# Batch 0 of a fused attention and feed-forward kernel: head groups share their last keys in pairs, and the load order changes

## The chip, the cores and the metric

One core of one Trainium2 chip. The metric is the device time of the whole program in microseconds. Three runs of the kernel before took 389.02, 389.39 and 390.98; the median is 389.39. The profiled execution took 389.4, and its span from the first to the last instruction is 387.6.

## What is computed

Softmax attention over 8 batches, 12 heads, 448 tokens and head size 64, then a feed-forward layer with SiLU on the tokens of all heads put side by side.

```python
scores = (1 / sqrt(64)) * q @ k.T          # per batch and head: 448 x 448
attn   = exp(scores - max) / sum           # softmax over the keys
x      = (attn @ v), heads side by side    # 3584 tokens x 768
h      = x @ w_in                          # 768 x 2048
g      = h / (1 + exp(-h))                 # SiLU
out    = g @ w_out                         # 2048 x 768, float32
```

## The kernel before, in words

**Units.** The 12 heads of a batch are three groups of four heads. For one group the keys and queries come in as one load each (`load_k`, L298, tile rk; `load_q`, L303, tile rq), 224 KB in float16, cast on the way by a DMA that POOL issues. VectorE turns both (`turn_k`, L347, tile KT; `turn_q`, L368, in place): 32 x 32 blocks are transposed, so that the head dimension lies on the partitions. The keys of a group lie in four chunks of up to 128.

**Score bursts.** `scores` (L419) multiplies one chunk of keys with the queries. Each head needs two matmuls of 32 rows (even and odd parts of the head dimension), so one burst is 8 matmuls of 448 queries on PE; heads run side by side on strips of 32 rows. The result s is 128 keys x 4 heads x 448 queries in PSUM, in two halves of two heads. `expo` (L439) turns each half into E with one exponential on ScalarE. Thus one burst gives two exponentials of 128 x 896.

**Lone and paired groups.** 448 keys are three and a half chunks. In a *lone* group (`LONES`, the first four: all of batch 0 and the first group of batch 1) the chunks have 128, 128, 96 and 96 keys, which makes four bursts. The other groups go in *pairs*: the first of a pair is "low", the second "high"; each has three chunks of 128 keys, and one burst takes the last 64 keys of both (`scores_rest`, L428: 16 matmuls with 64 key columns). A pair has seven bursts. In AV the shared E is read by both groups, with zeros in V in the 64 rows of the other one; POOL clears those rows (L323).

**Sums and AV.** For each group the sums of E over the keys (lone: matmuls with ones, `attend_part` L524 and `attend_wide` L494; pair: VectorE first adds three E into T, L455, then `attend_sums` L478) and two parts of E times V (16 matmuls of 32 columns each) go into PSUM tiles a. VectorE makes the inverse (`inverse`, L532: transpose sT, reciprocal, transpose rdn) and multiplies (`norm`, L567), which gives xT.

**Batch 0 in halves.** `BEGIN` lists the units of batch 0: group 0 with query columns 0 to 7 (of 14, 32 queries each), group 1 the same, group 2 whole, then the second halves of groups 0 and 1. A half unit packs two key chunks into one burst, so it has two bursts. As soon as all three groups have their first seven columns, the feed-forward of those tokens can start.

**Feed-forward.** `ffn1` (L609) makes h from xT and w_in, for batch 0 in two pieces of 224 tokens, six matmuls for each block of 128 columns of w_in; ScalarE makes tanh (L630), VectorE the gate G. Then batch 0's first products with w_out follow (o), and later batches go through sums of blocks with fewer products (p, f).

**What sets the order.** The kernel is written by a planner that runs when the program is built: class `Order` with a list of operations for each engine, their supposed durations, due times and rings of buffers. It decides which operation is written next on PE (a score burst, AV or feed-forward), and when nothing is ready in the first stage it writes filler: matmuls on a tile of zeros (`run_zeros`, L1618). The engines then run their own lists in order. The loads stand in one list on POOL, in the order of the `plan_...` calls; at most eight are in flight. There are 3 rk, 4 rq, 3 KT, 9 E and 2 V buffers, and 3 half-burst s tiles. Two PSUM banks hold sums and AV until batch 0's scores are done (`hand_over`), then four.

Of the kernel before, what the change touches and what calls it, by code (L numbers as in the profile page):

```python
# [20 lines left out]
OVERLAP = {"ACT": 0.09, "DVE": 0.07}  # L21
LOADS, DMA_SLOW = 8, 1.45
# [3 lines left out]
DMA_TAIL = 1.5  # L26
# [77 lines left out]
class Order:  # L104
# [48 lines left out]
    def step(self):  # L153
# [26 lines left out]
        elif self.pool:  # L180
# [9 lines left out]
            if at is not None and at <= self.now:  # L190
                self.pool.pop(0)
                if ring is not None:
                    ring.take()
                self.start(op)
                self.sent.append(op)
                took += DMA_SLOW if len(self.sent) == 3 else 0.0
                self.dma_free = max(self.dma_free, self.now + DMA_START) + took
                op.done = self.dma_free + DMA_TAIL
# [7 lines left out]
def kernel(  # L206
# [18 lines left out]
    KROWS = (128, 128, 96, 96)  # L225
    X_TOK = {
        "lone": ((0, 4), (4, 4), (8, 4), (12, 2)),
# [9 lines left out]
    LONES = (0, 1, 2, 3)  # L237
# [3 lines left out]
    NEAR, LATE = 0.15, -0.9  # L241
    COLD, FIRST = 8.5, 47
# [5 lines left out]
    WIDE_SUMS = True  # L248
    BEGIN = ((0, 0, 7), (1, 0, 7), (2, 0, 14), (0, 7, 14), (1, 7, 14))
    NB0 = len(BEGIN)  # L250
# [30 lines left out]
    for i in range(2):  # L281
        nc.vector.memset(both[64 * i : 64 * (i + 1)], 0.0)
        nc.vector.memset(both[64 * i : 64 * (i + 1), 16 * i : 16 * (i + 1)], 1.0)
    w_in_t = const.tile([128, NDC, DFF], FP16, name="w_in_t")
# [18 lines left out]
    def load_q(n):  # L303
        b, hg, g0, g1 = units[n]
        t = sb.tile([128, (g1 - g0) * D], FP16, name=f"rq_{n}", tag="rq", bufs=NRQ)
        nc.gpsimd.dma_start(out=t, in_=group_of(q, b, hg)[:, D * g0 : D * g1])  # L306
        rawq[n] = t

    def form(b, hg):
        n = NG * b + hg  # L310
        if n in LONES:
            return "lone"
        return ("low", "high")[(n - sum(x < n for x in LONES)) % 2]


    def load_v(b, hg0, hg1, x):
# [4 lines left out]
        if x == 0 and kind != "lone":  # L321
# [9 lines left out]


# [35 lines left out]
    def turn_q(n):  # L368
        t = rawq[n][:].bitcast(FP32).rearrange("p (g i) -> p g i", i=32)
# [33 lines left out]
    def score(pS, n, c, e, h, x0, x1, p0):  # L403
        b, hg, g0, g1 = units[n]
        nq = 32 * (g1 - g0)
        at = nq * (c % per_burst(n))
        nc.tensor.matmul(  # L407
            out=pS[p0 : p0 + 32 * (x1 - x0), h % 2, at : at + nq],
            lhsT=KT[(b, hg)][32 * h : 32 * (h + 1), c, x0:x1, :, e],
            rhs=QT[n][32 * h : 32 * (h + 1), e],  # L410
# [3 lines left out]

# [4 lines left out]
    def scores(n, w, ys):  # L419
        score_banks(n, w, ys)  # L420
        for c in range(per_burst(n) * w, per_burst(n) * (w + 1)):
            for e in range(2):
                for y in ys:
                    for h in (2 * y, 2 * y + 1):
                        score(pS_t[(n, w, y)], n, c, e, h, 0, rows_of(n, c) // 32, 0)


# [8 lines left out]
    def rows_of(n, c):  # L436
        return KROWS[c] if form(*units[n][:2]) == "lone" else 128

    def expo(n, w, y):  # L439
        kr = rows_of(n, w * per_burst(n))  # L440
        nk = 32 * (units[n][3] - units[n][2]) * per_burst(n)
        if (n, w) not in E:
            E[(n, w)] = sb.tile([128, HG, S], FP16, name=f"E_{n}_{w}", tag="E", bufs=NE)
        nc.scalar.activation(  # L444
            out=E[(n, w)][0:kr, 2 * y : 2 * y + 2, 0:nk],
            in_=pS_t[(n, w, y)][0:kr, :, 0:nk],
# [4 lines left out]

    def add_e(n, step):
        if step == 0:
            T[n] = sb.tile([128, HG, S], FP16, name=f"T_{n}", tag="T", bufs=NT_)
# [7 lines left out]
    def attend_mm(a, n, part, c, h, k0, k1, e, start, stop):  # L462
        b, hg, g0, g1 = units[n]
        nq = 32 * (g1 - g0)
        at = nq * (c % per_burst(n))
        if part == 0:
            w = ones[k0:k1, :]
        else:
            w = VT[b][k0:k1, HG * hg + h, c, part - 1 :: 2]
        nc.tensor.matmul(  # L470
            out=a[32 * h : 32 * (h + 1), 0:nq],
            lhsT=w,
            rhs=e[k0:k1, h, at : at + nq],
# [20 lines left out]
    def attend_wide(n):  # L494
        a = acc[(n, 0)] = psum_bank(f"a_{n}_0")
        for w in range(2):
            k = rows_of(n, 2 * w)
            for h in range(HG):
                nc.tensor.matmul(
                    out=a[32 * h : 32 * (h + 1), 0:S],  # L500
                    lhsT=ones[0:k, :],
                    rhs=E[(n, w)][0:k, h, 0:S],
                    start=(w == 0),
                    stop=(w == 1),
                )

    def attend(ns, part, n):
        if part == 0 and per_burst(n) == 2:
            attend_wide(n)
            return  # L510
        if part == 0 and len(ns) == 2:
            attend_sums(ns)
            return
        if part < 3:
            acc[(n, part)] = psum_bank(f"a_{n}_{part}")
        else:
            acc[(n, 3)] = acc[(n, 1)] = psum_bank(f"a_{n}_3")
            acc[(n, 2)] = acc[(n, 1)][:, 256:512]
            attend_part(ns, 1, n)
            attend_part(ns, 2, n)  # L520
            return
        attend_part(ns, part, n)

    def attend_part(ns, part, n):  # L524
        for c in range(NCH):
            e = E[(ns[0] if c == NCH - 1 else n, c // per_burst(n))]
            for h in range(HG):
                attend_mm(
                    acc[(n, part)], n, part, c, h, 0, rows_of(n, c), e, c == 0, c == NCH - 1
                )  # L530
# [1188 lines left out]
```

## Time and profile before

| | us |
|---|---|
| median of three runs | 389.39 |
| the profiled execution | 389.4 |
| its span | 387.6 |
| PE busy | 379.7 |
| DVE busy | 272.2 |
| ACT busy | 250.4 |
| POOL busy | 90.7 |

In the profile PE is TensorE, DVE is VectorE, ACT is ScalarE. A line of the page's slices has 40 digits, each the busy share of 9.7 us in tenths. A line of the timeline gives start, length, engine, line of the kernel, operation, tiles and shapes, and in brackets how long the engine was idle before it and what ended that. Matmuls overlap, so the lengths of neighbours on PE add up to more than the time from one start to the next; start to start is what a matmul costs. Tiles: rk and rq are raw keys and queries, KT turned keys, s scores, E exponentials, a sums and AV, xT the attention result, h and th the feed-forward, z the spare bank that filler writes.

### The profile page before, as it was taken

The page shows a single profiled execution, that of the slowest core. Times are in us where ns is not written, and L with a number is a line of the kernel's source. Part 1 is how long each engine was busy: PE and PEld are TensorE (multiplying, and loading weights), DVE is VectorE, ACT ScalarE, POOL GpSimd, SP SyncE. Part 2 cuts the span into 40 slices and gives each one's busy share as a digit, 9 for nine tenths or more (in the row PEclk, how much of TensorE's full clock was granted, in tenths as well). Part 3 has the DMA queues.
Part 4 walks back from the last instruction along what each step waited for, and adds up shares of the span by engine and source line. Part 5 has one row for each costly group of instructions (what it writes and reads, how often), then busy time and mean ns, then how long its engine had stood idle before and what let it go on. Part 6 is the DMA issues. An engine that isn't in the chain of part 4 may idle for free.

```text
span 387.6 us, 10639 instructions
## 1 busy us (share of the span) xinstructions
PE 379.7 (98%) x4374; PEld 198.8 (51%) x4374; DVE 272.2 (70%) x550; ACT 250.4 (65%) x383; POOL 90.7 (23%) x175
## 2 busy tenths in 40 slices
PE   8989999999999999999999999999999999999995
PEld 3548765444454444454455454554445655555663
DVE  2666768899985787978697658567769965447441
ACT  4988873787766879675955667566783248882220
POOL 7633366407006432502443024000000000000000
PEclk9999999999999999999999999999999999999999
DMA  7999999909148662924964139002000130001333
GB/s 115 199 210 209 166 159 214 202 5 126 20 102 121 126 85 34 155 57 84 149 91 56 42 82 160 4 3 65 20 1 2 43 100 23 0 2 41 91 96 101
DMA packets 36001, 34.52 MB, mean 89 GB/s; under 512 B 11376, under 2 KB 35184, under 8 KB 35952
## 3 DMA queue, kind: packets, MB, share of 16 engines
q0 software_dynamic: 25456, 22.82, 40.2%
q1 hardware_dynamic: 10080, 10.53, 10.1%
q8 instruction: 34, 0.56, 0.6%
q10 hardware_dynamic: 416, 0.49, 0.4%
q14 instruction: 15, 0.12, 0.1%
HBM read 45.61 MB, written 11.01 MB: 146 GB/s over the span
## 4 chain that ended last, share of the span: by engine, by line
PE 84%; DMA 12%; POOL 2%; issue 1%; DVE 1%; ACT 0%; POOLq 0%
PE p L598 31%; PE h L598 24%; PE s L407 8%; PE f L598 8%; PE a L470 8%; DMA rq<-in_q_dram 4%; DMA w_out_t<-in_moe_w_out_dram 3%; DMA rk<-in_k_dram 2%; DMA V<-in_v_dram 2%; PE a L486 2%; PE o L598 2%; POOL V L325 1%; POOL rk L300 0%; POOL rq L306 0%; POOL w_in_t L334 0%
## 5 line engine op out<-in xcount | busy, mean ns | idle before, releaser
L444 ACT ACTIVATE E<-s 128x896 f16<-128x896 f32 (+1 forms) x172 | 148.1, 915 | 31.1 <-PE s L407 30.4
L598 PE MATMUL h<-xT,w_in_t 128*32 128x448 f16 (+2 forms) x1338 | 117.2, 339 | 0.0
L598 PEld LDWEIGHTS <-w_in_t 128*32 128x32 f16 (+1 forms) x1410 | 71.8, 97 | 56.1 <-issue 11.6
L630 ACT ACTIVATE th<-h 128x448 f16<-128x448 f32 x96 | 52.3, 546 | 35.9 <-PE h L598 31.8
L598 PEld LDWEIGHTS <-G 128*128 128x128 f16 (+1 forms) x532 | 43.0, 98 | 33.2 <-issue 5.2
L889 ACT COPY ost<-p 128x384 f32<-128x384 f32 x52 | 25.0, 480 | 51.5 <-PE p L598 44.3
L674 DVE SCALAR_TENSOR_TENSOR G<-th,h 128x448 f16<-128x448 f16 (+1 forms) x80 | 44.1, 557 | 16.2 <-ACT th L630 15.8
L325 POOL DMA_DIRECT2D V<-in_v_dram x88 | 48.3, 560 | 15.5 <-DMA w_out_t<-in_moe_w_out_dram 6.1
L598 PE MATMUL p<-w_out_t,G 128*128 128x384 f16 (+1 forms) x304 | 49.1, 326 | 0.0
L407 PE MATMUL s<-rq,KT 32*128 32x448 f16 (+4 forms) x736 | 45.2, 345 | 1.5 <-DVE rq L378 1.3
L598 PEld LDWEIGHTS <-S 128*128 128x128 f16 (+1 forms) x384 | 29.8, 98 | 23.2 <-issue 3.1
L470 PE MATMUL a<-E,V 128*32 128x448 f16 (+3 forms) x800 | 39.9, 342 | 0.7 <-DVE sT L537 0.7
L306 POOL DMA_DIRECT2D rq<-in_q_dram x26 | 14.5, 557 | 101.6 <-PE s L407 89.4
L598 PE MATMUL p<-D,S 128*128 128x384 f16 (+1 forms) x256 | 36.8, 326 | 0.0
L895 DVE TENSOR_TENSOR ost<-p,ost 128x384 f32<-128x384 f32 x39 | 21.5, 552 | 14.5 <-PE p L598 12.4
L470 PEld LDWEIGHTS <-V 128*32 128x32 f16 (+1 forms) x832 | 20.7, 97 | 18.4 <-issue 6.1
L407 PEld LDWEIGHTS <-KT 32*128 32x128 f16 (+2 forms) x832 | 13.1, 98 | 29.9 <-issue 26.5
L586 DVE SCALAR_TENSOR_TENSOR xT<-a,rdn 128x448 f16<-128x448 f32 x44 | 26.4, 616 | 2.8 <-PE a L470 1.6
L455 DVE TENSOR_TENSOR T<-T,E 128x1792 f16<-128x1792 f16 x20 | 21.7, 1086 | 8.4 <-ACT E L444 8.4
L455 DVE TENSOR_TENSOR T<-E,E 128x1792 f16<-128x1792 f16 x20 | 21.7, 1083 | 8.3 <-ACT E L444 8.3
L360 DVE STREAM_TRANSPOSE KT<-rk 128x256 f32<-128x256 f32 (+3 forms) x48 | 16.5, 382 | 11.2 <-DMA rk<-in_k_dram 10.3
L598 PE MATMUL p<-w_out_t,S 128*128 128x384 f16 (+1 forms) x128 | 19.1, 327 | 0.0
(77 smaller groups left out, 333.4 us busy)
## 6 DMA issues: line engine op xcount, KB each, us to landing
out_dram<-ost SPq DMA_DIRECT2D x194, 48.0 KB, 1.6
rk<-in_k_dram POOLq DMA_DIRECT2D x24, 224.0 KB, 5.4
rq<-in_q_dram POOLq DMA_DIRECT2D x22, 224.0 KB, 5.2
w_out_t<-in_moe_w_out_dram POOLq DMA_DIRECT2D x4, 768.0 KB, 13.0
V<-in_v_dram POOLq DMA_DIRECT2D x43, 64.0 KB, 4.3
V<-in_v_dram POOLq DMA_DIRECT2D x40, 48.0 KB, 4.2
w_in_t<-in_moe_w_in_dram POOLq DMA_DIRECT2D x6, 256.0 KB, 7.5
w_in_t<-in_moe_w_in_dram POOLq DMA_DIRECT2D x3, 512.0 KB, 13.0
```

What stands on the lines that cost most here:

```text
L325: nc.gpsimd.dma_start(out=VT[b][32 * x : 32 * (x + 1), hs, 0:count, :], in_=v[b, hs].rearrange("h (i g) d -> i h g d", g=TPP)[:, :, first ...
L360: nc.vector.transpose(out=pairs[:, x:y, 0:count], in_=t[:, first : first + count * (y - x)].rearrange("p (x c) i -> p x c i", c=count),)
L407: nc.tensor.matmul(out=pS[p0 : p0 + 32 * (x1 - x0), h % 2, at : at + nq], lhsT=KT[(b, hg)][32 * h : 32 * (h + 1), c, x0:x1, :, e], rhs=QT[ ...
L444: nc.scalar.activation(out=E[(n, w)][0:kr, 2 * y : 2 * y + 2, 0:nk], in_=pS_t[(n, w, y)][0:kr, :, 0:nk], func=AF.Exp, scale=attn_scale,)
L455: nc.vector.tensor_tensor(out=T[n], in0=T[n] if step else E[(n, 0)], in1=E[(n, step + 1)], op=ALU.add,)
L470: nc.tensor.matmul(out=a[32 * h : 32 * (h + 1), 0:nq], lhsT=w, rhs=e[k0:k1, h, at : at + nq], start=start, stop=stop,)
L586: nc.vector.scalar_tensor_tensor(out=x3(b, cc)[:, cc % 3, 32 * g0 : 32 * g1], in0=acc[(n, part)][:, 0:nq], scalar=0.5, in1=rdn_t[n].rearra ...
L598: nc.tensor.matmul(out=out[i : i + cut], lhsT=w[:, i : i + cut], rhs=x, start=start, stop=stop, skip_group_check=True,)
L630: nc.scalar.activation(out=th, in_=h_t[(b, f, t0)][:, 0:n], func=AF.Tanh)
L674: nc.vector.scalar_tensor_tensor(out=dst[:, f, at + lo : at + hi], in0=th_t[(b, f, t0)][:, lo - t0 : hi - t0], scalar=1.0, in1=h_t[(b, f, ...
L889: nc.scalar.copy(out=ost(qd, *OUT[m]), in_=bank(qd, BANK[m]))
L895: nc.vector.tensor_tensor(out=t, in0=bank(qd, BANK[m]), in1=t, op=ALU.add)
```

## The change

- **Pairs from the start.** There are no lone groups any more. Groups 0 and 1 of batch 0 are a pair, and so are group 2 of batch 0 and group 0 of batch 1. A table, `BURSTS`, lists the bursts of these four: each entry is a pair of (chunk, half of the queries). Groups 0 and 1 are whole units; group 0's fourth burst holds the last keys of both. Its first two bursts hold chunks 0 and 1 for the first and then the second half of the queries, so its first exponentials need only the first half of q, which is loaded in two pieces.
- **Group 2 in query halves.** Its bursts are: chunks 0 and 1 for the first half, chunks 2 and 3 for the first half, then the same for the second half. Chunk 3 is shared with group 0 of batch 1, whose keys and queries are therefore loaded earlier. Sums, AV and inverse of group 2 run for each half.
- **Sums.** In these four groups the sums are matmuls with ones, and for the shared chunk with `side`, which has ones in one half of the rows.
- **E of the first two bursts** goes into the tile T, with a reordered view, instead of an E buffer.
- **V of batch 0** is loaded in the "low" form for all three groups in one set of four loads. VectorE clears the upper 64 rows of the last chunk at the start (`first_v`); for group 1 it copies the lower 64 rows to the upper ones and clears the lower (`lift_v`).
- **Loads.** V of batch 0 comes ahead of the third group's queries; keys and queries of batch 1's first two groups come ahead of w_in's blocks; V groups of batch 1 and the third and fourth w_out loads alternate.
- **Planner constants** change (`DMA_LATE`, `DMA_MORE`, `DMA_TAIL`, `LATE`, `QUIET`), which shift what it writes where. Filler is written only for a wait above 0.16 instead of 0.06.

On the engines this makes 168 exponentials of 128 x 896 elements instead of 172, 29 filler matmuls instead of 48, and on PE the same count of AV and sum columns.

```diff
-    KROWS = (128, 128, 96, 96)
     X_TOK = {
-        "lone": ((0, 4), (4, 4), (8, 4), (12, 2)),
         "low": ((0, 4), (4, 4), (8, 3), (11, 3)),
         "high": ((0, 3), (3, 3), (6, 4), (10, 4)),
     }
...
-    LONES = (0, 1, 2, 3)
...
-    NEAR, LATE = 0.15, -0.9
-    COLD, FIRST = 8.5, 47
+    NEAR, LATE = 0.15, -0.3
+    COLD, FIRST, QUIET = 8.5, 47, 0.16
...
-    BEGIN = ((0, 0, 7), (1, 0, 7), (2, 0, 14), (0, 7, 14), (1, 7, 14))
-    NB0 = len(BEGIN)
+    BURSTS = (
+        (((0, 0), (1, 0)), ((0, 1), (1, 1)), ((2, 0), (2, 1)), ((3, 0), (3, 1))),
+        (((0, 0), (0, 1)), ((1, 0), (1, 1)), ((2, 0), (2, 1))),
+        (((0, 0), (1, 0)), ((2, 0), (3, 0)), ((0, 1), (1, 1)), ((2, 1), (3, 1))),
+        (((0, 0), (0, 1)), ((1, 0), (1, 1)), ((2, 0), (2, 1))),
+    )
+    PASSES = {1: (3, 0, 1, 2)}
+    ALONE = len(BURSTS)
+    NB0 = 3
...
+    def first_v():
+        VT[0] = sb.tile([128, NH, NCH, D], FP16, name="V_0", tag="V", bufs=2)
+        nc.vector.memset(VT[0][64:128, :, NCH - 1, :], 0.0)
...
+    def lift_v(step):
+        hs = slice(HG, 2 * HG)
+        if step == 0:
+            nc.vector.tensor_copy(
+                out=VT[0][64:128, hs, NCH - 1, :], in_=VT[0][0:64, hs, NCH - 1, :]
+            )
+        else:
+            nc.vector.memset(VT[0][0:64, hs, NCH - 1, :], 0.0)
...
     def scores(n, w, ys):
         score_banks(n, w, ys)
-        for c in range(per_burst(n) * w, per_burst(n) * (w + 1)):
+        for c, q0, q1, at in strips_of(n, w):
             for e in range(2):
...
+                for h in range(HG):
+                    pS = pS_t[(n, w, h // 2)]
+                    if c < NCH - 1:
+                        score(pS, n, c, e, h, 0, 4, 0, q0, q1, at)
+                        continue
+                    x = 0 if form(*units[n + 1][:2]) == "low" else 2
+                    score(pS, n, c, e, h, 0, 2, 0, q0, q1, at)
+                    score(pS, n + 1, c, e, h, x, x + 2, 64, q0, q1, at)
...
     def expo(n, w, y):
...
+        if n == 0 and w < 2:
+            E[(0, w)] = TT[:, w]
+            at = S // 2 * w
+            nc.scalar.activation(
+                out=TT[:, :, 2 * y : 2 * y + 2, at : at + S // 2],
+                in_=pS_t[(n, w, y)][:, :, 0:S].rearrange("p h (c q) -> p c h q", c=2),
...
     plan_k(0, 2)
+    plan_v(0, 0, NG)
     plan_q(2)
-    plan_v(0, 0, NG)
+    plan_k(1, 0)
     plan_q(3)
+    plan_w_in(0, 512)
+    plan_w_in(512, 1024)
+    plan_k(1, 1)
     plan_q(4)
-    plan_w_in(0, DFF // 4)
-    plan_w_in(DFF // 4, DFF // 2)
-    plan_k(1, 0)
-    plan_q(NB0)
-    plan_w_in(DFF // 2, DFF)
-    plan_k(1, 1)
-    plan_q(NB0 + 1)
-    plan_w_out(0, NFF // 4)
-    plan_w_out(NFF // 4, NFF // 2)
+    plan_w_in(1024, 2048)
     plan_k(1, 2)
-    plan_q(NB0 + 2)
-    for hg in range(NG):
-        plan_v(1, hg, hg + 1)
-    plan_w_out(NFF // 2, 3 * NFF // 4)
-    plan_w_out(3 * NFF // 4, NFF)
+    plan_q(5)
+    plan_w_out(0, 4)
+    plan_w_out(4, 8)
+    plan_v(1, 0, 1)
+    plan_w_out(8, 12)
+    plan_v(1, 1, 2)
+    plan_w_out(12, 16)
+    plan_v(1, 2, 3)
```

More of the change, by code (lines that the diff above doesn't have):

```diff
@@ L1012, in leave_bank @@
         return lambda at: m_ring.give(at, bank_of[name])
+    lift = []
+    for step, busy in ((0, 0.35), (1, 0.2)):
+        lift.append(
+            od.add(Op("DVE", busy, lambda step=step: lift_v(step), ld_v[(0, 1)] + lift[-1:], -5))
+        )
     moe = []
@@ L1481, in run_qk @@
         op.half = len(ys) == 1
-        if c == NCH // per_burst(n) - 1 and ys[-1] == 1:
-            done = []
-            for m in ns:
-                if last_unit[units[m][:2]] == m:
-                    done.append(kt_ring)
-                done.append(rq_ring)
+        done = [kt_ring, rq_ring] * len(ns)
+        if rest or n < ALONE and c == len(BURSTS[n]) - 1:
             op.then = lambda at: [r.give(at) for r in done]
-        od.on_pe(op, "rest rows" if rest else "rows", 16 if rest else 4 * per_burst(n) * len(ys))
+        kind = "rest rows" if pieces[-1][0] == NCH - 1 else "rows"
+        od.on_pe(op, kind, count)
         for y in ys:
@@ L1527, in av_at @@
         ns, part, n = av_seq[0]
-        if len(ns) == 2 and part == 0:
+        if part == 0 and not alone(n):
             if any(len(t_op.get(x, ())) < 2 for x in ns):
```

313 lines of the change are left out of this document (182 added, 131 removed).

## Prediction

> **What bounds the kernel now.** I read the head of the page first, then the slices, then busy time by stage, then the timeline of the first 75 us.
>
> ```profile
> span 387.6 us, 10639 instructions
> PE 379.7 (98%) x4374; PEld 198.8 (51%) x4374; DVE 272.2 (70%) x550; ACT 250.4 (65%) x383; POOL 90.7 (23%) x175
> ...
> PE   8989999999999999999999999999999999999995
> ...
> ACT  4988873787766879675955667566783248882220
> ...
> DMA  7999999909148662924964139002000130001333
> ```
>
> TensorE is busy for 98% of the span, but that average mixes stages. The busy time by stage (stretch, length, PE busy, then PEld, DVE, ACT, POOL, granted clock, DMA share, GB/s) separates them:
>
> ```profile
> 6.00:24.00 18.00, 16.91 (x313) 9.19 (x302) 9.91 (x24) 16.98 (x21) 10.28 (x17) 1.00 1.26 197
> 24.00:34.00 10.00, 8.81 (x158) 6.30 (x155) 6.34 (x16) 7.97 (x11) 3.56 (x6) 1.00 1.13 210
> 72.00:388.00 316.00, 311.72 (x3414) 157.34 (x3406) 227.43 (x451) 199.22 (x315) 51.35 (x101) 1.00 0.38 68
> ```
>
> After 72 us TensorE is the bound: 311.7 of 316. Whatever is won ahead of that point, or taken from TensorE, reaches the end one for one. From 6 to 24 us ScalarE is the bound (16.98 of 18); much of what PE does there is filler, the matmuls on zeros. DMA is full until about 60 us. The timeline shows how the stages hand over (start, length, engine, line, operation; in brackets the idle time before and what ended it):
>
> ```profile
> 6.38 15.24 ACT L444 ACTIVATE E<-s 128x896 f16<-128x896 f32 x18 [4.35 <-PE s L407]
> 23.57 0.75 PE L598 MATMUL h<-xT,w_in_t 128*128 128x224 f16 x6
> 26.75 0.96 PE L470 MATMUL a<-E,V 128*32 128x224 f16 x32 [0.72 <-DVE sT L537]
> 28.17 0.57 PE L407 MATMUL s<-rq,KT 32*128 32x448 f16 x8 [0.47 <-DVE rq L378]
> 28.68 0.56 PE L499 MATMUL a<-E,ones 128*32 128x448 f16 x8
> 29.95 1.32 PE L598 MATMUL h<-xT,w_in_t 128*128 128x224 f16 x12
> 34.12 0.60 PE L407 MATMUL s<-rq,KT 32*96 32x448 f16 x8
> 34.65 2.47 PE L598 MATMUL h<-xT,w_in_t 128*128 128x224 f16 x24
> 37.05 0.60 PE L407 MATMUL s<-rq,KT 32*96 32x448 f16 x8
> 39.42 0.94 PE L470 MATMUL a<-E,ones 128*32 128x448 f16 x16
> 40.29 0.57 PE L407 MATMUL s<-rq,KT 32*128 32x448 f16 x8
> 57.01 2.11 PE L598 MATMUL o<-w_out_t,G 128*128 128x384 f16 x12 [0.37 <-DMA w_out_t<-in_moe_w_out_dram]
> 60.76 1.46 PE L598 MATMUL o<-w_out_t,G 128*128 128x384 f16 x8 [0.36 <-DMA w_out_t<-in_moe_w_out_dram]
> 72.19 2.44 PE L598 MATMUL h<-xT,w_in_t 128*128 128x448 f16 x12
> ```
>
> Read it as three parts. ScalarE runs 18 exponentials back to back in 15.24 us, 0.847 each. At 23.57 the first feed-forward matmul (h) starts; from there PE always has something to do, and loses only four waits: 0.72, 0.47, 0.37 and 0.36, together 1.92. At 72.19 the feed-forward of batch 1 starts. I call 23.57 the handover and 72.19 the mark.
>
> **Prices on PE, start to start.** A score burst costs 34.65 - 34.12 = 0.53. An h matmul of 224 columns costs (37.05 - 34.65)/24 = 0.10. A pass of 16 matmuls (sums, or one part of AV) costs 40.29 - 39.42 = 0.87. Sums and AV of one half of the queries cost 29.95 - 28.68 = 1.27.
>
> **The change part by part.**
>
> *Shared keys.* Four groups with four bursts each (16) become two pairs with seven (14), so two score bursts and four exponentials go. A shared burst issues 16 matmuls of 64 key columns instead of 8, two side by side. Before already does this for later groups, and the burst at 59.05 costs the same 0.53 to the next start:
>
> ```profile
> 59.05 0.60 PE L407 MATMUL s<-rq,KT 32*64 32x448 f16 x16
> 59.58 0.82 PE L598 MATMUL o<-w_out_t,G 128*128 128x384 f16 x4
> ```
>
> Sums and AV keep their columns; some matmuls become two of half the width. So PE loses 2 x 0.53 = 1.06 of work for certain.
>
> *The handover.* Before needs 16 exponentials for the first seven query columns of all three groups (4 + 4 + 8). After needs 8 + 6 + 4 = 18, as groups 0 and 1 now come whole and only group 2 in halves. That is 6.38 + 18 x 0.847 = 21.63. Then comes the chain of a half unit: sums (about 0.25), transpose, reciprocal, transpose, product. Its rows (operation, shape, count, then busy us and mean ns):
>
> ```profile
> L556 DVE STREAM_TRANSPOSE rdn<-inv 128x224 f32<-128x224 f32 x4 | 1.6, 411 | 0.1
> L552 DVE RECIPROCAL inv<-sT 128x7 f32<-128x7 f32 x4 | 0.8, 201 | 0.1
> L575 DVE SCALAR_TENSOR_TENSOR xT<-z,rdn 128x448 f16<-128x448 f32 x1 | 0.6, 625 | 0.0
> ```
>
> 0.25 + 0.41 + 0.20 + 0.41 + 0.62 = 1.9, and about 0.4 for four hand-offs: 2.3. Before's chain took 23.57 - (6.38 + 16 x 0.847) = 3.64, because it was 448 wide throughout. One thing starts later: the second burst reads the second half of the first queries, the third load, where before it used the half it had.
>
> ```profile
> 5.34 0.37 DVE L378 STREAM_TRANSPOSE rq<-rq 128x224 f32<-128x224 f32 x1
> 8.01 0.70 DVE L360 STREAM_TRANSPOSE KT<-rk 128x384 f32<-128x384 f32 x2 [2.31 <-DMA rk<-in_k_dram]
> 9.73 0.70 DVE L360 STREAM_TRANSPOSE KT<-rk 128x384 f32<-128x384 f32 x2 [0.67 <-DMA rk<-in_k_dram]
> ```
>
> The third load of before, 224 KB, landed at 8.0. Half as many bytes take about 0.55 less (a load of 224 KB takes 1.1, see below): 7.45. Then 0.41 to turn it and 0.67 from the end of that to the exponential (5.71 to 6.38): 8.5, where the first burst's exponentials end at 8.1. I take 0.4 late; the ends are 0 and 1.0 (if it lands no sooner than the larger load). Handover: 21.63 + 0.4 + 2.3 = 24.3.
>
> *What is left of PE's work at the handover.* Before, from handover to mark: 48.62, less the waits of 1.92, is 46.70. In the order of the built program, before issues 14 score bursts in that stretch and after 11: 3 x 0.53 = 1.59. Before also has two half units of sums and AV left, after one: 1.27. The h and o matmuls are the same. So 46.70 - 1.59 - 1.27 = 43.84 is left, and the mark stands at 24.3 + 43.84 = 68.1 without waits. That is 4.05 sooner; one of the three bursts (0.53) is only moved behind the mark. **Gain without new waits: 3.5.** It holds the 1.06; the rest is the time at which ScalarE held PE up, and before's four waits.
>
> *New waits.* After puts keys and queries of the next two groups ahead of the last w_in blocks. POOL keeps eight loads in flight, so its waits tell landings:
>
> ```profile
> 15.08 0.92 DVE L378 STREAM_TRANSPOSE rq<-rq 128x224 f32<-128x224 f32 x2 [2.62 <-DMA rq<-in_q_dram]
> 19.77 0.70 POOL L334 DMA_DIRECT2D w_in_t<-in_moe_w_in_dram  x1 [0.58 <-DMA w_in_t<-in_moe_w_in_dram]
> 34.23 0.55 POOL L325 DMA_DIRECT2D V<-in_v_dram  x1 [1.93 <-DMA w_in_t<-in_moe_w_in_dram]
> 35.37 0.54 POOL L325 DMA_DIRECT2D V<-in_v_dram  x1 [0.58 <-DMA rk<-in_k_dram]
> 36.44 0.54 POOL L325 DMA_DIRECT2D V<-in_v_dram  x1 [0.52 <-DMA rq<-in_q_dram]
> 40.19 0.54 POOL L325 DMA_DIRECT2D V<-in_v_dram  x1 [2.87 <-DMA w_out_t<-in_moe_w_out_dram]
> ```
>
> A load of 224 KB takes 1.1 (35.37 to 36.44), one of w_out 3.75. The third group's second burst now needs two loads behind those of 15.1: 17.3, and turned (0.70 + 0.65, behind other work on DVE) by about 18.9; ScalarE asks for it at 6.38 + 0.4 + 15 x 0.847 = 19.5. The first quarter of w_in lands at 19.8 + 2.2 = 22.0, ahead of the handover. The last w_in block landed just ahead of 34.2; two more loads ahead of it make 36.3. PE first needs that block after 78 h matmuls, four score bursts, one half unit and one sums pass: 24.3 + 7.8 + 2.12 + 1.27 + 0.87 = 36.4. The margin is nil; a late landing stalls PE and all that is queued behind on it. I take 0.3, with ends 0 and 1.5. The third and fourth w_out loads now stand ahead of two and of one group of V rows, so they land sooner than the 57.0 and 60.7 that PE waited for, and those waits go; the V rows of batch 1 have the same bytes ahead as before. For waits such as the 0.72 and 0.47 (a PSUM bank not yet read, a transpose queued behind others on DVE) I take 0.4, from nothing to 1.2.
>
> *V rows on VectorE.* A copy and two clears, 64 rows each, of which one clear comes ahead of the first keys in DVE's idle time. No row shows such a copy: it lies between the 0.20 of the reciprocal and the 0.62 of a 448-wide product. It stands in DVE's order between the transpose and the reciprocal of group 0, and waits there for V; the product, and the bank that it frees, wait behind it. ScalarE's chain of exponentials covers that; without cover it would cost up to 0.6. Nothing is taken.
>
> *Exponentials written through a reordered view* (the first four). No row shows them; two half instructions of the nearest kind would take 2 x 0.546 each against 0.847:
>
> ```profile
> L630 ACT ACTIVATE th<-h 128x448 f16<-128x448 f32 x16 | 8.7, 546 | 2.2 <-PE h L598 2.0 <-ACT th L630 0.2
> ```
>
> So 0 to 1.0 for all four, on the path to the handover. I take 0, as the elements and the instruction count are the same.
>
> Sum: 3.5 - 0.3 - 0.4 = 2.8. The profiled execution took 389.4, which is the median (389.39) too: **386.6**.
>
> **Rivals.** *(a) The early gain is swallowed.* Handover a microsecond later (the upper ends above) and bank waits as long as before's: only the two score bursts remain, 389.4 - 1.06 = 388.3. For it: the first bursts hang on a load that was not theirs before, and every group of the first three now has a full-width or later chain. Against it: the exponentials are 0.847 apart whatever is behind them, and PE has slack there.
>
> *(b) The load queue is late: slower.* Place: PE's first use of the upper half of w_in. Every microsecond beyond 36.4 goes to the end. From 36.4 + 3.1 = 39.5 on the kernel is slower than before; 41.5 would give 391.4. For it: the DMA share is 1.26 and 1.13 in the rows of the first 34 us, and four loads are moved ahead. Against it: the rows above space loads evenly, and I count 36.3.
>
> *(c) The clock.* Filler is cut, and the clock could fall.
>
> ```profile
> L1623 PE MATMUL z<-zeros x48: 218/278/635, 1.0 to 18.8; 128*128 128x512 f16 x16, 128*128 128x128 f16 x16, 128*128 128x256 f16 x13, 128*128 128x384 f16 x3
> ...
> 6.00:9.40 3.40, 2.78 (x54) 1.00 1.11 175
> ```
>
> Before issues 48 fillers, after 29 (12 at the start in both). At half clock PE's work from 13 us to the handover (six passes, six bursts, a half unit: 9.7) would take 19 instead of fitting in 11: about 8 later, 394. The row shows 1.00 granted where PE was busy 2.78 of 3.4. The Trainium skill (TensorE: Matmul & The Clock Gate, What's actually happening) says that an idle window of about 3.4 us halves the clock. By that rule nothing happens here, as score bursts come every 1.7 us; the trace agrees so far as it never shows less than 1.00.
>
> **How the numbers follow.** Forecast 0.62, 385.2 to 387.4. Rival (a) 0.26, 387.5 to 389.4. Rival (b) 0.08, half of it above 391.3. Rival (c) 0.04. A measurement tells about 0.5% from no change, that is below 387.45 or above 391.35: faster 0.62, same 0.30, slower 0.08. Range 385.2 (no new wait, 0.4 not lost, and a little more) to 389.4: it holds the forecast and (a).
>
> **What would show it.** Right: about 168 E exponentials; the second burst's start near 8.5; first h near 24.3; the 448-wide h near 68 to 69; no w_out wait; 1.00 granted throughout. Wrong: a w_in wait of PE near 36 above 1 us, a gap in ScalarE's chain between 15 and 22 us, or a busy share after the mark that is lower than 311.7 of 316.

## The result, and the profile after

The changed kernel takes 385.28 us (median of 5 runs, 384.91 to 385.70), the kernel before 389.42 (5 runs). The ratio is 0.9887, with a 95% interval of 0.9865 to 0.9908: 1.1% faster. 386.6 was forecast, with a range of 385.2 to 389.4. The direction was right, and so was the mechanism of the gain; its size was not: the gain is 4.1 where 2.8 was forecast. By the ratio, 0.9887 of 389.39 is 385.0, just outside the range.

| us | before | forecast | after |
|---|---|---|---|
| median | 389.42 | 386.6 | 385.28 |
| profiled execution (span) | 389.4 (387.6) | | 385.3 (383.5) |
| first exponential | 6.38 | 6.38 | 6.88 |
| handover (first h) | 23.57 | 24.3 | 24.06 |
| handover to mark | 48.62 | 43.84 + 0.7 of waits | 43.22 |
| mark (first 448-wide h) | 72.19 | 68.8 | 67.28 |
| mark to end of span | 315.44 | 0.5 more | 0.8 more |

The same lines of the page's head as before (span; busy time by engine; slices):

```profile
span 383.5 us, 10780 instructions
PE 378.2 (99%) x4454; PEld 196.7 (51%) x4454; DVE 270.5 (71%) x546; ACT 246.8 (64%) x379; POOL 90.4 (24%) x175
...
PE   8999999999999999999999999999999999999995
...
ACT  4987862987766878576946666467784248881220
...
DMA  7999999919049752824964258003000131001333
```

They say little: PE is busy for 1.5 us less and the span is 4.1 shorter. The third digit of the PE row, from 19 to 29 us, went from 8 to 9; that is where the two longest waits were. The busy time by stage of the kernel after shows it better (stretch, length, busy time of PE, PEld, DVE, ACT, POOL, granted clock, DMA share, GB/s):

```profile
6.00:24.00 18.00, 17.52 (x319) 7.69 (x319) 11.25 (x27) 16.41 (x20) 10.14 (x16) 1.00 1.24 199
24.00:34.00 10.00, 10.00 (x147) 8.03 (x145) 6.27 (x13) 8.46 (x13) 4.23 (x8) 1.00 1.14 211
72.00:388.00 316.00, 307.64 (x3482) 155.64 (x3481) 222.49 (x444) 196.13 (x310) 49.11 (x97) 0.99 0.36 65
```

From 24 to 34 us PE now works without a hole (10.00 of 10, before 8.81). The last stretch ends at 383.5, so 307.6 of 311.5 are busy there, the share that it had before (311.7 of 315.6). The timeline of the kernel after, first the stage of attention, then the handover, the load that POOL issues once the last w_in block has landed, the w_out blocks and the mark:

```profile
6.88 3.35 ACT L471 ACTIVATE T<-s 128x896 f16<-128x896 f32 x4 [4.85 <-PE s L426]
7.76 0.67 PE L426 MATMUL s<-rq,KT 32*128 32x224 f16 x16 [0.36 <-DVE rq L399]
10.09 9.86 ACT L480 ACTIVATE E<-s 128x896 f16<-128x896 f32 x12
14.88 0.22 DVE L348 COPY V<-V 64x256 f16<-64x256 f16 x1
20.45 3.34 ACT L480 ACTIVATE E<-s 128x896 f16<-128x896 f32 x4 [0.50 <-PE s L426]
24.06 1.38 PE L646 MATMUL z<-xT,w_in_t 128*128 128x224 f16 x12
36.27 0.55 POOL L337 DMA_DIRECT2D V<-in_v_dram  x1 [1.92 <-DMA w_in_t<-in_moe_w_in_dram]
53.21 2.12 PE L646 MATMUL o<-w_out_t,G 128*128 128x384 f16 x12
55.80 2.12 PE L646 MATMUL o<-w_out_t,G 128*128 128x384 f16 x12
67.28 1.30 PE L646 MATMUL h<-xT,w_in_t 128*128 128x448 f16 x6
```

What to see: the rows of PE from 24 us on carry no bracket. All four waits of before are gone (0.72, 0.47, 0.37, 0.36), and none came in their place; 0.36 at 7.76, ahead of the handover, is the one wait that is left. The two w_out rows stand where before waited at 57.01 and 60.76. The four exponentials with the reordered write (line 471) go to the next one in 10.09 - 6.88 = 3.21, 0.80 each, so the reordering costs nothing that shows. The copy of the V rows takes 0.22.

**Where the 4.1 comes from.** Ahead of the handover 0.5 is lost, between handover and mark 5.40 is won (48.62 to 43.22), behind the mark 0.82 is lost again, of which 0.53 is the score burst that was moved there.

### The profile page after: what moved, and what is told of

Same layout as the page of the kernel before. It is cut to its first block, busy times and chain, and to the rows that moved or that the text cites. A ratio compares the mean times of both kernels' runs of the same rounds, so it can differ in the third digit from the quotient of the medians.

```text
span 383.5 us, 10780 instructions
## 1 busy us (share of the span) xinstructions
PE 378.2 (99%) x4454; PEld 196.7 (51%) x4454; DVE 270.5 (71%) x546; ACT 246.8 (64%) x379; POOL 90.4 (24%) x175
## 4 chain that ended last, share of the span: by engine, by line
PE 97%; DMA 1%; POOL 0%; issue 0%; ACT 0%; DVE 0%; POOLq 0%
PE p L646 31%; PE h L646 29%; PE s L426 12%; PE a L544 8%; PE f L646 8%; PE o L646 3%; PE a L530 2%; PE a L560 2%; DMA rq<-in_q_dram 1%; PE z L1708 1%; PE z L646 0%; PE z L530 0%; POOL rk L310 0%; POOL rq L318 0%; ACT ost L937 0%
## 5 line engine op out<-in xcount | busy, mean ns | idle before, releaser
L480 ACT ACTIVATE E<-s 128x896 f16<-128x896 f32 x164 | 141.2, 923 | 24.5 <-PE s L426 23.9
L646 PE MATMUL h<-xT,w_in_t 128*32 128x448 f16 (+2 forms) x1308 | 116.0, 340 | 0.0
L678 ACT ACTIVATE th<-h 128x448 f16<-128x448 f32 x95 | 51.9, 546 | 36.3 <-PE h L646 33.1
L426 PE MATMUL s<-rq,KT 32*128 32x448 f16 (+3 forms) x728 | 45.2, 347 | 0.5 <-DVE rq L399 0.4
L544 PE MATMUL a<-E,V 128*32 128x448 f16 x640 | 33.9, 353 | 0.0
L634 DVE SCALAR_TENSOR_TENSOR xT<-a,rdn 128x448 f16<-128x448 f32 x46 | 27.7, 616 | 3.4 <-PE a L544 1.7
L426 PEld LDWEIGHTS <-KT 32*128 32x128 f16 (+1 forms) x824 | 12.6, 96 | 30.3 <-issue 27.8
L544 PEld LDWEIGHTS <-V 128*32 128x32 f16 x640 | 15.7, 97 | 16.3 <-issue 5.3
L381 DVE STREAM_TRANSPOSE KT<-rk 128x256 f32<-128x256 f32 (+1 forms) x48 | 16.4, 380 | 5.0 <-DMA rk<-in_k_dram 4.8
```

Source lines behind the costliest of these rows:

```text
L381: nc.vector.transpose(out=pairs[:, x:y, 0:count], in_=t[:, first : first + count * (y - x)].rearrange("p (x c) i -> p x c i", c=count),)
L426: nc.tensor.matmul(out=pS[p0 : p0 + 32 * (x1 - x0), h % 2, at : at + q1 - q0], lhsT=KT[(b, hg)][32 * h : 32 * (h + 1), c, x0:x1, :, e], rh ...
L480: nc.scalar.activation(out=E[(n, w)][:, 2 * y : 2 * y + 2, :], in_=pS_t[(n, w, y)][:, :, 0:S], func=AF.Exp, scale=attn_scale,)
L544: nc.tensor.matmul(out=a[32 * h : 32 * (h + 1), 0:S], lhsT=VT[b][:, HG * hg + h, c, part - 1 :: 2], rhs=e[:, h], start=start, stop=stop,)
L634: nc.vector.scalar_tensor_tensor(out=x3(b, cc)[:, cc % 3, 32 * g0 : 32 * g1], in0=acc[(n, part)][:, 0:nq], scalar=0.5, in1=rdn_t[n].rearra ...
L646: nc.tensor.matmul(out=out[i : i + cut], lhsT=w[:, i : i + cut], rhs=x, start=start, stop=stop, skip_group_check=True,)
```

## The experiments

They were timed in three series; "control" is the unedited kernel in one of them, together with the whole third group, the kernel without the turns and the one without filler. The kernel before took 389.24 in that series, and 389.27 and 389.06 in the two others. Every ratio is to the kernel before, with its 95% interval. Where spans are compared, they are those of one profiled execution each.

### The control: the changed kernel again

> The changed kernel once more, unedited, as the yardstick for the runs beside it. Both theories: 385.3, within 0.4; first feed-forward matmul (the handover) near 24.1, first 448-wide one (the mark) near 67.3. It also shows how far the landing of the first query load (5.77 here, 5.27 in the kernel before) moves from one profile to the next.

Measured: 385.2 us, ratio 0.9901 [0.9886, 0.9916]; span 383.4, handover 23.93, mark 67.15. The result repeats, and no PE wait stands between handover and mark here either.

### The third group's queries whole

```diff
-        (((0, 0), (1, 0)), ((2, 0), (3, 0)), ((0, 1), (1, 1)), ((2, 1), (3, 1))),
+        (((0, 0), (0, 1)), ((1, 0), (1, 1)), ((2, 0), (2, 1)), ((3, 0), (3, 1))),
```

(and one count of E buffers that are given back).

> The changed kernel with the third group's queries whole again: its four bursts hold one chunk each for all queries, so the first half of the feed-forward needs 22 exponentials instead of 18. Theory (the end follows the handover, less what PE can do meanwhile): handover 4 x 0.847 = 3.4 later and a chain 0.9 longer, about 28.3; PE has about 2.6 of other work for that time, so 1.7 more at the end, 387.0. Rival (the early stage has slack, the gain comes from less PE work and fewer waits): within 0.4 of 385.3.

Measured: 387.25 us, ratio 0.9952 [0.9938, 0.9966]. The timeline of this kernel:

```profile
28.29 2.47 PE L646 MATMUL h<-xT,w_in_t 128*128 128x224 f16 x24
70.22 2.43 PE L646 MATMUL h<-xT,w_in_t 128*128 128x448 f16 x12
```

The handover comes 4.36 later than in the control (23.93), and the end 2.05 later. Half of the delay comes back, because PE does other work in the meantime. The early handover, that is the halves of the third group, is worth about 2 us, half of the gain.

### Two more exponentials ahead of the handover

```diff
-                    lambda y=y: expo(n, c, y),
+                    lambda y=y: [expo(n, c, y) for _ in range(1 + (n == 1 and c == 1))],
```

(with the planner told of twice the duration; the two are the second group's, computed twice.)

> The changed kernel with one burst's two exponentials of the second group computed twice (same values): 1.7 more of ScalarE ahead of the handover and nothing more on PE. Theory (ScalarE's chain sets the handover, and PE has nothing else to do): handover 1.7 later, end 1.2 to 1.7 later, 386.5 to 387.0. Rival (slack): within 0.4 of 385.3.

Measured: 386.86 us, ratio 0.9941 [0.9929, 0.9953], 1.66 above the control. The first h of this kernel:

```profile
25.49 2.07 PE L646 MATMUL h<-xT,w_in_t 128*128 128x224 f16 x18
```

Two exponentials of some 0.83 move the handover by 1.56 and the end by 1.66. Time on ScalarE ahead of the handover goes to the end one for one, as the prediction priced it.

### Two score bursts more behind the handover

```diff
-        for c, q0, q1, at in strips_of(n, w):
+        for c, q0, q1, at in strips_of(n, w) * (1 + (n in (4, 5) and w == 1)):
```

(Two bursts of batch 1 are computed twice, into the same tile; the planner is told.)

> The changed kernel with two score bursts of batch 1 (second and third group) computed twice, after the handover: 16 more matmuls on PE, no more exponentials. Theory (PE is the bound from the handover on): 0.37 to 0.53 each, 0.75 to 1.06 in all, 386.0 to 386.4. Rival (PE's burst is hidden behind ScalarE): within 0.3 of 385.3.

Measured: 385.87 us, ratio 0.9921 [0.9907, 0.9935], 0.67 above the control. This is just below the theory's band. The two intervals overlap, but all six runs of this kernel are above 385.6 and four of the control's five below. The timeline of this kernel shows one doubled burst between two groups of h:

```profile
38.61 0.97 PE L426 MATMUL s<-rq,KT 32*128 32x448 f16 x16
39.51 2.47 PE L646 MATMUL h<-xT,w_in_t 128*128 128x224 f16 x24
```

A doubled burst takes 39.51 - 38.61 = 0.90 to the next start, a single one in the control 0.51. So eight more matmuls behind eight of their kind cost 0.39, and the visit as such (a change from h to scores and back) about 0.12. PE is the bound there, and a burst that disappears with its visit is worth 0.51 to 0.53, as in the sum.

### Before, with only the turns of V and w_out

The edit is made in the kernel before: its V loads of batch 1 and its third and fourth w_out loads take turns, and nothing else changes.

```diff
-    for hg in range(NG):
-        plan_v(1, hg, hg + 1)
+    plan_v(1, 0, 1)
     plan_w_out(NFF // 2, 3 * NFF // 4)
+    plan_v(1, 1, 2)
     plan_w_out(3 * NFF // 4, NFF)
+    plan_v(1, 2, 3)
```

> The kernel before with one part of the change alone: V groups of batch 1 and the third and fourth w_out load take turns. Theory (each w_out wait of before costs its start-to-start excess, 0.44 and 0.52): both go, 0.96 sooner, 388.4. Rival (the turn-taking carries more, through what the planner then puts first): 387.9 or less. Third: no difference, 389.4.

Measured: 388.25 us, ratio 0.9977 [0.9966, 0.9988]: 1.0 faster than before. Both w_out waits are gone from its timeline. The turns alone bring a quarter of the gain. The place of the mark doesn't show this: it is 72.65, and the stretch behind it is 1.6 shorter than in the kernel before, as the planner writes AV, o and score bursts in another order there. This profile also tells something of the two early waits of before. In the same work, before any w_out load is needed, it has a single wait of 0.34 in place of 0.72 and 0.47, because the keys that VectorE turns ahead of that place landed sooner (turned at 24.91 instead of 25.46). So these two waits differ from one execution to the next.

### The changed kernel without the turns

```diff
     plan_v(1, 0, 1)
-    plan_w_out(8, 12)
     plan_v(1, 1, 2)
-    plan_w_out(12, 16)
     plan_v(1, 2, 3)
+    plan_w_out(8, 12)
+    plan_w_out(12, 16)
```

> The changed kernel with the old load order at one place: all V groups of batch 1 ahead of the third and fourth w_out load. Theory (the gain beyond the forecast is waits that did not come, and the old waits were dearer than their idle time): w_out lands 2.2 and 1.1 later (two and one V groups of 1.1 each), about 52.9 and 56.9, where PE now asks for it at 53.2 and later, so 385.3 to 386.3. Rival (the turn-taking of the loads carries what the forecast missed): 386.7 or more.

Measured: 386.47 us, ratio 0.9929 [0.9914, 0.9944], 1.27 above the control, which falls between the two bands. Only 0.33 of it is a wait that the timeline of this kernel shows:

```profile
60.51 2.11 PE L646 MATMUL o<-w_out_t,G 128*128 128x384 f16 x12 [0.33 <-DMA w_out_t<-in_moe_w_out_dram]
69.96 2.44 PE L646 MATMUL h<-xT,w_in_t 128*128 128x448 f16 x12
```

The planner knows of the later loads and writes o, AV and score bursts in another order: the mark stands 2.8 later and the stretch behind it is 1.6 shorter. So this run confirms that the turns are worth about a microsecond in this kernel too, but does not tell how much of it is waiting and how much is the other order.

### V of batch 0 by groups, as it would be without the move on VectorE

```diff
-        return "low" if b == 0 else ("low", "high")[(NG * b + hg) % 2]
+        return ("low", "high")[(NG * b + hg) % 2]
...
-    plan_v(0, 0, NG)
+    for hg in range(NG):
+        plan_v(0, hg, hg + 1)
...
-    for step, busy in ((0, 0.35), (1, 0.2)):
+    for step, busy in ():
```

Group 1 takes the "high" form straight from memory, so the V of batch 0 comes in twelve loads of 64 and 48 KB in place of four of 192 and 144 KB; POOL clears the rows. The bytes are the same.

> The changed kernel with V of batch 0 loaded by group in the form that each group needs (12 loads instead of 4, POOL clears the rows), so nothing is moved on VectorE. Theory: the move itself is hidden, and what it buys is eight issues of 0.55 on POOL and places among the eight loads in flight; the third group's queries and the next keys come 1 to 2 later, ScalarE waits that long, 386.3 to 387.3. Rival (the bytes are the same and the DMA queue is full either way): 385.3, within 0.4.

Measured: 391.73 us (8 runs, 389.60 to 394.06), ratio 1.0062 [1.0037, 1.0086]: slower than before, 6.5 above the control, and much more than I expected. The runs fall in two groups: four with a mean clock of 0.998 or 0.999 took 389.60 to 391.20, and four with 0.991 to 0.995 took 392.26 to 394.06. So 4.4 to 6.0 is lost without a fall of the clock that shows in the mean, and more with one; the profiled execution (392.26) is of the second group. The busy time by stage, and the timeline, of this kernel:

```profile
6.00:24.00 18.00, 16.98 (x244) 7.21 (x244) 9.72 (x21) 13.68 (x17) 13.02 (x25) 1.00 1.08 151
34.00:48.00 14.00, 14.00 (x149) 10.65 (x148) 8.65 (x18) 9.79 (x15) 4.23 (x8) 0.88 1.14 210
```

```profile
20.37 1.73 ACT L479 ACTIVATE E<-s 128x896 f16<-128x896 f32 x2 [1.72 <-PE s L425]
23.60 3.35 ACT L479 ACTIVATE E<-s 128x896 f16<-128x896 f32 x4 [1.50 <-PE s L425]
27.25 1.33 PE L645 MATMUL z<-xT,w_in_t 128*128 128x224 f16 x12
...
32.58 0.70 DVE L380 STREAM_TRANSPOSE KT<-rk 128x256 f32<-128x256 f32 x2 [4.97 <-DMA rk<-in_k_dram]
33.21 0.58 DVE L712 SCALAR_TENSOR_TENSOR G<-th,z 128x448 f16<-128x448 f16 x1
33.84 0.73 PE L645 MATMUL h<-xT,w_in_t 128*128 128x224 f16 x6 [2.23 <-DVE G L712]
35.02 4.67 PE L645 MATMUL h<-xT,w_in_t 128*128 128x224 f16 x30
75.05 2.43 PE L645 MATMUL h<-xT,w_in_t 128*128 128x448 f16 x12
```

Read the chain from the left: between 6 and 24 us the loads move 151 GB/s, where the kernel after has 199. At most eight loads are in flight, and small ones hold the places: the third group's queries are issued at 13.93 instead of 7.55. They and the next group's keys and queries land at 18.2, 20.4 and 21.5 (after: 15.8, 16.9, 18.6), so ScalarE stands still for 1.72 and 1.50, and the handover is 3.3 later. Behind it the next keys land late as well. VectorE has their turn in its order ahead of a gate, and stands before it for 4.97 us (32.58); the gate's other input, the tanh, was done at 29.40. The gate then runs at 33.21, and only then is the PSUM tile free that the h at 33.84 writes: PE has waited 2.23. So a load is felt three engines away, through the order of VectorE. The last w_in block lands at 40.95 (after: 35.98), and nobody waits for it, because all else is late. Then the 30 h matmuls at 35.02 take 4.67 instead of 3.05, because the clock is 0.5 for 3.4 us behind the wait, which the stage's mean of 0.88 shows. The Trainium skill (DMA: Bandwidth & Descriptors, Rules for kernel authors) says to coalesce many small transfers, and that below 64 KB one pays mostly overhead. This run points the same way, with loads at and just below that size; what it shows is the places in flight that they hold, not the overhead of a single load.

### The move on GpSimd instead

```diff
-            nc.vector.tensor_copy(
+            nc.gpsimd.tensor_copy(
...
-            nc.vector.memset(VT[0][0:64, hs, NCH - 1, :], 0.0)
+            nc.gpsimd.memset(VT[0][0:64, hs, NCH - 1, :], 0.0)
```

> The copy and the clearing of the second group's V rows (lines 348 and 352) run on GpSimd in place of VectorE; the first values still come in one set of four loads. Theory (what the move buys is the four full loads in place of twelve small ones, and any engine with time to spare can move the rows): VectorE saves 0.22 + 0.17 us and POOL, which issues the loads, spends about 1 us more between w_in loads; the last w_in block may land up to 1 us after 35.98, and it has 0.2 us to spare, so 385.1 to 386.1 us, handover within 0.2 us of 23.93. Rival (the queue of loads on POOL can bear no wait for the values to land, since everything issued behind the copy waits too): w_in and w_out later by 1 us or more, a wait on the ffn's h at 36 us, 386.3 us or more.

Measured: 385.54 us, ratio 0.9909 [0.9896, 0.9923], the control's within its interval; handover 23.93. The timeline of POOL in this kernel:

```profile
14.79 0.39 POOL L348 COPY V<-V 64x256 f16<-64x256 f16 x1
15.13 0.70 POOL L355 DMA_DIRECT2D w_in_t<-in_moe_w_in_dram  x1
15.87 0.30 POOL L352 MEMSET V<- 64x256 f16 x1
```

The last w_in block lands at 36.08 instead of 35.98. The engine does not matter; what is worth 6.5 us in the median is that the rows are moved on the chip at all, so that V comes in four large loads. (The run by groups also has POOL clear three more blocks of rows; the 0.39 and 0.30 that POOL spends here change nothing that shows, so those clears are hardly the cause.)

### Without filler, and with half of it

Filler (line 1708) is left out after the first twelve blocks in the first kernel:

```diff
-        if warm["on"] and not dark and od.free["PE"] <= od.now and wait > QUIET and od.now > 0.9:
+        if warm["on"] and not dark and od.free["PE"] <= od.now and wait > (QUIET if "first" not in warm else 0.16) and od.now > 0.9:
```

(with QUIET at 50 instead of 0.16), and each of those fillers is cut to half its length in the second:

```diff
-            od.on_pe(Op("PE", n * each, lambda n=n, wide=wide, i=m_ring.free[0][1]: run_zeros(n, wide, i)), "full", -(-n // wide))
+            od.on_pe(Op("PE", n * each, lambda n=n if n == FIRST else -(-n // 2), wide=wide, i=m_ring.free[0][1]: run_zeros(n, wide, i)), "full", -(-n // wide))
```

> The changed kernel without any filler matmul after the first twelve. Theory: score bursts every 1.7 us keep the clock at 1.00, PE has slack before the handover: 385.3, within 0.4. Rival (the filler is what holds the clock): granted clock below 1.00 between 8 and 24 us, handover 1 us or more later, 386.3 or more.

Measured: 386.76 us, ratio 0.9935 [0.9921, 0.995], 1.56 above the control. The profiled execution took 386.30, 1.10 above the control's.

> Every filler after the first twelve blocks is cut to half its length, in the same places. Theory (the granted clock goes by how much of a window of some 3.4 us TensorE works, and the line lies between the 2.98 busy of 3.40 us with clock 1.00 of the changed kernel and the 1.94 of 3.40 us behind which the clock fell to 0.5 without filler; this kernel lies at about 2.2 to 2.5): I put 0.6 on the clock holding, with 385.1 to 385.7 us and handover 23.9; 0.4 on its falling for 3.4 us or more between 9 and 16 us, with 386.0 to 387.0 us. Rival (only a stretch wholly without work lowers the clock): 385.3 us and clock 1.00 throughout, for here as without filler no such stretch is over 1.2 us; but the run without filler already speaks against it.

Measured: 385.23 us, ratio 0.9907 [0.9893, 0.992], like the control.

Busy time in windows of 3.4 us, of the kernel after, then without filler, then with half of it, and last of the kernel before, around its waits of 0.72 and 0.47. The first number after the comma is PE, the third from the right the granted clock:

```profile
5.90:9.30 3.40, 2.98 (x41) 1.45 (x41) 1.20 (x4) 2.42 (x4) 1.74 (x3) 1.00 1.09 183
9.30:12.70 3.40, 3.36 (x33) 1.09 (x31) 1.57 (x4) 3.40 (x6) 2.05 (x4) 1.00 1.42 188
```

```profile
5.90:9.30 3.40, 1.94 (x39) 0.95 (x40) 1.10 (x3) 2.63 (x4) 1.89 (x4) 1.00 1.10 184
9.30:12.70 3.40, 3.21 (x28) 0.80 (x29) 1.36 (x4) 3.40 (x5) 1.99 (x4) 0.51 1.37 179
12.70:16.10 3.40, 3.40 (x34) 0.72 (x32) 0.92 (x3) 2.33 (x4) 2.45 (x4) 0.50 1.24 207
```

```profile
5.90:9.30 3.40, 3.00 (x40) 1.41 (x40) 0.88 (x3) 2.24 (x3) 1.75 (x3) 1.00 1.09 184
6.80:10.20 3.40, 2.69 (x38) 1.04 (x31) 1.21 (x4) 3.14 (x4) 1.40 (x3) 1.00 1.15 186
9.30:12.70 3.40, 2.96 (x31) 0.85 (x29) 1.80 (x5) 3.40 (x6) 1.95 (x4) 1.00 1.44 188
```

```profile
25.80:29.20 3.40, 2.21 (x59) 1.27 (x60) 3.25 (x9) 2.14 (x4) 1.21 (x2) 1.00 1.13 213
```

Without filler PE works 1.94 of 3.40 us, and then the clock is 0.5 for 6.8 us. The busy time that follows is no sign of health: 3.21 and 3.40 are the same work at half speed. ScalarE runs out of scores:

```profile
15.96 4.96 ACT L480 ACTIVATE E<-s 128x896 f16<-128x896 f32 x6 [1.07 <-PE s L426]
```

That is 1.07, about the 1 us by which the handover is late (24.92). With half the filler PE falls to 2.69 of 3.40 (6.80 to 10.20) and the clock holds. I had put that kernel at 2.2 to 2.5; filler that is cut left less of a hole than I thought. The kernel before has the emptiest window behind which the clock held: 2.21. If it is the busy share of such a window that counts, the line lies between 1.94 and 2.21 of 3.40. These runs do not show that it is the share: the two windows also hold different kinds of matmul.

None of the edits gave a kernel faster than the changed one; half the filler equals it.

## Why the prediction fell short, and what in it was right

**The handover: right, by terms that cancel.** Forecast 6.38 + 0.4 + 15.25 + 2.3 = 24.3, measured 24.06. The first exponential came 0.50 later; between the profiles of this study it lies anywhere from 6.38 to 7.06, with the first loads' landing, and is no work of the change. The second burst, which I had 0.4 late, waited (0.36, on the turn of the second half of the queries), but ScalarE saw no gap, because its own start was as late. The 18 exponentials end at 20.45 + 2 x 3.34 / 4 = 22.12, which is 15.24 after the first, the 0.50 gap included. So without the gap an exponential took 0.82, where I had 0.847; why is open. From there the first h came 24.06 - 22.12 = 1.94 later, for 2.3. The chain itself was no shorter: its product runs from 23.84 to 24.47, which ends 2.35 after the exponentials. But the first four of the six matmuls of an h block read only groups 0 and 1 (`ffn1` takes the rows of w_in in the order of the heads), so h starts about 0.4 ahead of the product's end. The gap of 0.50 is the one place where a load ordered by the change makes itself felt: the next group's queries landed at 18.6, not 17.3, and their burst started at 19.70. The prediction had named a gap in ScalarE's chain between 15 and 22 us as a sign that it was wrong; this one came, and the shorter exponentials paid for it.

**The work between handover and mark: right.** By kinds of matmul, start to start, score bursts lost 2.05 of which 0.44 is the wait that stood behind one of them (1.61 left; forecast 1.59), and sums and AV lost 1.92 of which 0.55 is a wait (1.37 left; forecast 1.27).

**The step that failed: "New waits".** I took 0.3 for w_in and 0.4 for banks and VectorE, 0.7 in all. The runs show 0: neither came in the changed kernel, nor in the control or any edit that keeps its order of loads. The last w_in block landed at 35.98 (forecast 36.3), and the first h that reads the upper half of w_in started at 36.18 (forecast 36.4). The margin looks like 0.2, but it is about 0.6: the upper half comes in three loads, by rows, and the last of them holds the rows for the fifth and sixth matmul of a block, 0.4 later. I had taken the block's start for its need.

For the 0.4 I had argued from before's kind of wait, without asking what caused it. In the kernel before it was a late load, felt through the order of VectorE:

```profile
25.46 0.70 DVE L360 STREAM_TRANSPOSE KT<-rk 128x384 f32<-128x384 f32 x2 [1.84 <-DMA rk<-in_k_dram]
26.09 0.61 DVE L537 STREAM_TRANSPOSE sT<-a 128x448 f32<-128x448 f32 x1
27.52 0.60 DVE L378 STREAM_TRANSPOSE rq<-rq 128x448 f32<-128x448 f32 x1
```

VectorE stands 1.84 before the keys of batch 1's first group; the sums' transpose (sT), for which PE waits 0.72, comes behind them, and so do the queries, for which PE waits 0.47. The change loads these keys and queries earlier, since they now belong to a pair with the third group, and both are turned ahead of the handover:

```profile
17.98 0.69 DVE L381 STREAM_TRANSPOSE KT<-rk 128x192 f32<-128x192 f32 x2
18.64 0.65 DVE L399 STREAM_TRANSPOSE rq<-rq 128x448 f32<-128x448 f32 x1
```

So the change takes away the cause of the waits whose like I charged. No run moves these two loads alone.

**Mis-sized: before's four waits.** I valued them at their idle time, 1.92. From start to start they cost 2.30: the group of six h ahead of the first took 1.47 instead of 0.68 (0.79 for 0.72), the score burst ahead of 57.01 took 0.95 instead of 0.51 (0.44 for 0.37), and the other two 0.55 and 0.52. An idle gap counts from the modelled end of a matmul, and the overlap with the next one is lost as well.

**The balance.** 2.8 forecast, + 0.7 for the waits that didn't come, + 0.38 for the old waits, + 0.24 less from fewer changes between kinds of matmul, + 0.24 for the handover, - 0.28 behind the mark: 4.08 of 4.1. The 0.24 of changes is what is left of the difference, so the sum had to close; that it is the changes was argued from the count of visits, not tried. And before's first two waits, 1.34 of the 2.30, are those of one execution. What the 0.28 behind the mark is stays open. It is not the clock: the 0.99 of the last stage comes from the end, where PE has no work left (380.00 to 383.50: busy 0.00, clock 0.76). Nor is it idle time of PE, whose busy share behind 72 us is the one of before; the prediction had named a lower share as a sign that it was wrong.

**V rows on VectorE: cost right, worth not seen.** "Nothing is taken" holds: the copy takes 0.22 under ScalarE's chain. That the four large loads which it makes possible are worth 6.5 us in the median beside twelve small ones, I did not see, because the kernel before also loads V of batch 0 in four loads: there all groups have one form. Pairs need two forms, and the copy is what keeps the four loads.

**Rival (a)** didn't happen: no bank wait stands behind the handover. **Rival (b)** didn't happen in the changed kernel, but the run with V by groups shows that a late queue of loads can make the kernel slower, and by another way than I named: not at w_in, but through the late queries (ScalarE), the late keys (VectorE) and then the clock.

**Rival (c): its chance was about right, its reasoning wrong.** The clock held, with 26 filler matmuls (not 29, as I had counted). But I had said that by the rule nothing would happen, as bursts come every 1.7 us. Without filler the second and third bursts came 1.4 and 1.0 us apart, no pause of PE between 6 and 16 us was longer than 0.79 us, and the clock fell to 0.5. So the rule of the idle window, as I read it, does not protect a kernel that works in short pieces. The same page of the Trainium skill (TensorE: Matmul & The Clock Gate, A second HAM failure mode: psum-queue depth-cycling) tells of a kernel whose frequent short pauses made the clock swing; the run without filler is of that kind, with pauses of 0.79, 0.23 and 0.44 us ahead of one fall of the clock. Some of the filler that remained was needed (half of it was enough), and the price without it is 1.56 us, not 8, since the clock recovered before the handover.

## What to carry to other kernels

When a stage ahead of the bound is shortened, price the waits that disappear by start to start. When the margin of a load comes out as nil, look for the single instruction that is first to read it. Before you charge a new wait by the size of an old one, find what caused the old one, and whether the change leaves that cause in place. Ask of every small piece of on-chip work that a change adds which loads it keeps large: with a fixed number of loads in flight, twelve of 48 and 64 KB in place of four large ones cost 48 GB/s over 18 us and 4.4 to 8.9 us here. Before filler is cut, look at the busy share per 3.4 us beside one that held the clock, and not at the longest pause alone.

## What the runs showed of the hardware that was not expected

- The clock fell to 0.5 after a window in which PE worked 1.94 of 3.40 us, with no pause over 0.79 us; it held behind 2.21 of 3.40 in the kernel before (25.80 to 29.20, pauses of 0.72 and 0.47) and 2.69 with half the filler.
- After a wait of 2.23 us on PE in the run with V by groups the clock was 0.5 for 3.4 us, and 30 h matmuls took 4.67 instead of 3.05. In four of that kernel's eight runs the mean clock was 0.991 to 0.995.
- An exponential with a reordered write (four pieces of 224 elements a row, put apart) took no longer than a plain one: 0.80 from start to start.
- The first exponential's start differs by 0.7 us between the profiled executions (6.38 to 7.06), with the landing of the first loads.
